# Key exponentials taken by ScalarE from PSUM with the maximum as bias, in the feature map of a linear-attention and mixture-of-experts kernel

## The chip, the cores and the metric

One Trainium2 chip, one core of it. The metric is the device time of one execution in microseconds (us); the median of several executions is given. A profiled execution is a separate one and has a time of its own. TensorE (PE) multiplies matrices and writes to PSUM, VectorE (DVE) and ScalarE (ACT) read PSUM, GpSimd (POOL) works in SBUF and issues indirect transfers, SyncE (SP) issues the other transfers. Each engine runs its own list of instructions in order; semaphores tie the lists together.

## The reference

```
def phi(x):
    proj = np.einsum('bhsd,df->bhsf', x, w_phi)
    proj = proj - np.max(np.abs(proj), axis=-1, keepdims=True)
    return np.concatenate([np.exp(proj), np.exp(-proj)], axis=-1)
q_p, k_p = (phi(q), phi(k))
kv = np.einsum('bhsf,bhsd->bhfd', k_p, v)
z = np.sum(k_p, axis=2)
num = np.einsum('bhsf,bhfd->bhsd', q_p, kv)
den = np.einsum('bhsf,bhf->bhs', q_p, z)[..., None] + 1e-06
x = (num / den)          # then, token by token: a router over 8 experts,
...                      # h = relu(x @ w1[e]); out = p[e] * (h @ w2[e])
```

Batch 8, 8 heads, 576 tokens, head dimension 64, 128 features; the model dimension is 512, there are 8 experts with a hidden width of 1024. Everything is fp32. For each token and head the kernel thus needs the maximum of the absolute projections, and four sets of 128 exponentials: of the shifted projection and of its negative, for q and for k.

## The kernel before

The first stage is the attention. Two batches and two heads form a unit of 9 chunks of 128 tokens (1152 tokens, of which chunk 4 holds tokens of both batches); there are 16 units. The stage runs in 72 steps of two chunks each. Step p, in the function `step`, does on TensorE, in this order (the TensorE order of this stage is the order of the code; a scheduler sets that of the other engines):

- `proj(p)`: 8 matmuls (16 instructions each of weight load and matmul in the profile, since fp32 takes two) give the projections of k and q, two heads and two chunks, into a tile `pj` of two PSUM banks, one bank for each head. There are two such tiles in turn. VectorE then takes the maximum of absolute values (`m`, 8 columns) and subtracts it (`sb`), ScalarE takes the key features `kp` as two exponentials.
- `qtr(p-1)`: 8 instructions transpose the shifted q of the step before, `sb`, back into the same `pj` tile; ScalarE turns that into the query features `qp` (`qexp`), 2 exponentials.
- turns: where a sum over keys was finished in the step before, 4 more transposes of it (`kvs`) into the same tile; ScalarE copies them to `ks`.
- `kv4` (chunk 4 alone), gates, `kv`: the keys' features times v are summed into `kvp`. Where such a sum is complete, ScalarE copies it to `kvs` (`kv_end`). A gate, one step after a turn, is 8 instructions of TensorE and a small ScalarE copy into `kvs`.
- up to 18 entries of the list `todo`: the numerators and denominators `nm`, which VectorE divides (`rc`, `xo`).

Spread over the later steps are the router's steps, transfers that POOL issues behind a small copy named `tick`, and in the last of the 72 steps eight splits of expert weights (a ScalarE cast to `whi`, then four POOL subtractions to `wlo`). After the 72 steps come the experts' layers, for which TensorE is nearly always busy.

In the listing below and in all profile rows of the kernel before, line 277 is the projections, 280 the maximum, 282 the subtraction, 286 the key exponentials, 295 the transposes, 310 the query exponentials, 327 and 340 the sums over keys, 361, 362 and 385 the copies into `kvs`, 374 the copy to `ks`, 405 the numerators.

Of the kernel before, what the change touches and what calls it, by code (L numbers as in the profile page):

```python
# [7 lines left out]
F32 = mybir.dt.float32  # L8
# [3 lines left out]
AF = mybir.ActivationFunctionType  # L12
ALU = mybir.AluOpType
AX = mybir.AxisListType
# [12 lines left out]
MID, DEN = slice(10, 10 + 2 * D), slice(9, 11 + 2 * D, 2 * D + 1)  # L27
# [28 lines left out]
class Kernel:  # L56
# [209 lines left out]
    def proj(self, p):  # L266

        dve, act = self.dve, self.act

        t = self.psf.tile([128, 2, 2, 2, 128], F32, name="pj")  # L270
        for i in (2 * p, 2 * p + 1):
            kq = self.g[i // 3]["kq"]
            s = slice(i % 3 * 128, i % 3 * 128 + 128)
            for j in (0, 1):
                for h in (0, 1):
                    r = slice(64 * h, 64 * h + 64)
                    self.last_pe = self.pe.matmul(t[:, h, i % 2, j, :], kq[r, j, s], self.w2[r], start=True, stop=True)  # L277
        m = self.m = self.front3.tile([128, 8], F32, name="m")
        f = t.rearrange("p h c j f -> p (h c j) f")
        dve.tensor_reduce(m, f, AX.X, ALU.max, apply_absolute_value=True)  # L280
        sb = self.front3.tile([128, 2, 2, 2, 128], F32, name="sb")
        self.last_dve = dve.tensor_sub(sb.rearrange("p h c j f -> p (h c j) f"), f,  # L282
                                       m.unsqueeze(2).broadcast_to([128, 8, 128]))
        kp = self.front3.tile([128, 2, 2, 2, 128], F32, name="kp", bufs=4)
        for sg in (0, 1):
            self.last_act = act.activation(kp[:, :, :, sg, :].rearrange("p c h f -> p h c f"), sb[:, :, :, 0], AF.Exp,  # L286
                                           scale=1.0 - 2 * sg)
        for c in (0, 1):
            self.ch[2 * p + c] = dict(kp=kp[:, c], sb=sb, pj=t.rearrange("p h c j f -> p h (c j f)"))

    def halves(self, t, a, src):

# [4 lines left out]
    def qtr(self, p):  # L297

        sb, pj = self.ch[2 * p]["sb"], self.ch[2 * p]["pj"]
        for h in (0, 1):  # L300
            for c in (0, 1):
                self.halves(pj, h * 128 + c * 64, sb[:, h, c, 1, :])
        return pj

    def qexp(self, p, pj):

        qp = self.feat.tile([128, 2, 2, 256], F32, name="qp")
        src = pj[:, :, 0:256].rearrange("p r (a k) -> p a r k", k=64)
        for sg in (0, 1):
            self.act.activation(qp[:, sg].rearrange("p h (c r k) -> p (h c) r k", c=2, r=2), src, AF.Exp,  # L310
                                scale=1.0 - 2 * sg)
        for c in (2 * p, 2 * p + 1):
            self.ch[c]["qp"] = qp
# [41 lines left out]
    def kv_end(self, u, b, t):  # L355


        hp = u % NHP
        kvs = self.back2.tile([128, 2, 2 * (KV + D + 1)], F32, name="kvs", bufs=3)
        with self.tc.high_priority():  # L360
            self.act.copy(kvs[:, :, MID].rearrange("p s (h d) -> p s h d", h=2), t[:, :, :, 0:D])
            self.act.copy(kvs[:, :, DEN], t[:, :, :, D])
        e = {}

        def turn(t):
            for sg in (0, 1):
                self.halves(t, 256 + sg * 64, kvs[:, sg, MID])
            self.gates.append(gate)
            return copy

        def copy(t):
            e["ks"] = self.back2.tile([128, 2, 128], F32, name="ks")
            with self.tc.high_priority():
                self.act.copy(e["ks"].rearrange("p s (r k) -> p s r k", r=2),
                              t[:, :, 256:384].rearrange("p r (s k) -> p s r k", s=2))

        def gate():

            t = self.psb.tile([128, 512], F32, name="nm")
            g = t[:, 476:512].rearrange("p (s h e) -> p s h e", s=2, h=2)  # L380
            for sg in (0, 1):
                for r in (slice(0, 64), slice(64, 128)):
                    self.pe.matmul(g[r, sg], e["ks"][:, sg, r], self.wgi[:, hp], start=True, stop=True)
            with self.tc.high_priority():
                self.act.copy(kvs.rearrange("p s (h x) -> p s h x", h=2)[:, :, :, 0:9], g)
            for k, cs in enumerate(((0, 1), (2, 3)) if b == 0 else ((4, 5, 6), (7, 8))):
                self.num(u, b, cs, kvs, None if k else t)
            if b == 1 and hp == NHP - 1:
                self.todo.append(lambda: self.ends(u // NHP))
        self.turns.append(turn)  # L390

    def num(self, u, b, cs, kvs, bank=None):
# [92 lines left out]
    def step(self, p, n):  # L485

        if p < n // 2:
            self.proj(p)
        gates, self.gates = self.gates, []
        turns, self.turns = self.turns, []  # L490
        q = 0 <= p - 1 < n // 2
        if q:
            pj = self.qtr(p - 1)
        elif turns:
            pj = self.psf.tile([128, 2, 512], F32, name="pj")
        copies = [x(pj) for x in turns]
        if q:
            self.small_ps = [pj[:, r, 384:512] for r in (0, 1)]
        self.chores()
        if q:  # L500
            self.qexp(p - 1, pj)
        for x in copies:
            x(pj)
        pair = (2 * (p - KVLAG), 2 * (p - KVLAG) + 1) if 0 <= p - KVLAG < n // 2 else ()
        for i in pair:
            if i % NC == 4:
                self.kv4(i)
        for x in gates:
            x()
        for i in pair:  # L510
            if i % NC != 4:
                self.kv(i)
        for _ in range(min(QUOTA, len(self.todo)) if p < n // 2 else len(self.todo)):
            self.todo.pop(0)()
# [523 lines left out]
    def tokens(self, slots, late=False):  # L1038

        for s in slots:  # L1040
            if "xg" not in s:
                self.gather_x(s)
        units, g = [(s, k) for s in slots for k in range(s["n"])], 1 if late else 4

        def step(group):
            if late:
                self.whole(*group[0], group[0][1] % 3 == 2, self.here())
                return
            out = []
            for n, (s, k) in enumerate(group):  # L1050
                if n % 2 == 0:
                    t = self.halfbanks()
                c = slice(n % 2 * 256, n % 2 * 256 + 256)
                out.append((s, k, t[:, :, c]))
                self.rows(out[-1][2], s["xg"][k])
            for s, k, t in out:
                self.unrow(s, *self.into(s), k * 128, t)
        return [lambda a=a: step(units[a:a + g]) for a in range(0, len(units), g)]
# [295 lines left out]
```

## Time and profile before

| | |
|---|---|
| median of 3 executions | 752.32 us (751.82 to 754.76) |
| profiled execution, its time | 757.47 us |
| profiled execution, its span | 755.6 us |
| TensorE matmul busy | 730.0 us, 97% of the span |
| VectorE busy | 452.1 us, 60% |
| ScalarE busy | 341.4 us, 45% |
| POOL busy | 181.7 us, 24% |
| granted TensorE clock, mean | 0.996 |
| first and last projection matmul start | 4.2 us and 284.1 us |

The profiled execution is 5.2 us (0.7%) above the median. Shares are averages over two different stages: the attention up to about 285 us, the experts after that. A row of the timeline gives start, length, engine, line, operation and tiles; PEld is TensorE's weight load, which precedes its matmul and overlaps others; idle time before a row and what ended it stand in brackets.

### The profile page before, as it was taken

How to read it: one execution, taken by the hardware profiler on the slowest of the kernel's cores; microseconds unless marked ns; L12 is line 12 of the kernel's file. 1: busy time of each engine (PE TensorE's matmuls, PEld its weight loads, DVE VectorE, ACT ScalarE, POOL GpSimd, SP SyncE). 2: the span in 40 equal slices, each digit the busy share in tenths (PEclk: the TensorE clock that was granted, in tenths of full speed). 3: DMA queues.
4: the chain of work that ended last, by engine and by line, in shares of the span. 5: the costliest groups of instructions: out<-in, count | busy, mean ns of one | idle time of the engine just before them, and what ended most of it. 6: DMA issues, size and time to landing. Idle time of an engine off the chain costs nothing. (4 is left out here: it accounts for less than half of the span.)

```text
span 755.6 us, 22152 instructions
## 1 busy us (share of the span) xinstructions
PE 730.0 (97%) x9447; PEld 632.3 (84%) x9447; DVE 452.1 (60%) x828; ACT 341.4 (45%) x644; POOL 181.7 (24%) x306
## 2 busy tenths in 40 slices
PE   7999999999998899989999999999999999999996
PEld 6999989989887788869887985889888778888995
DVE  5888888788877886583736335435522365543513
ACT  4777666666677574322424225332322255251301
POOL 0210103410364674344403130021212102101011
PEclk9999999999999999999999999999999999999999
DMA  6755545554666651054737966434686264334110
GB/s 203 239 170 146 150 128 148 136 153 129 196 194 195 197 163 54 7 170 142 262 120 284 333 249 203 164 126 140 237 299 239 98 233 167 139 126 154 57 39 29
DMA packets 66101, 125.05 MB, mean 166 GB/s; under 512 B 7220, under 2 KB 45300, under 8 KB 65950
## 3 DMA queue, kind: packets, MB, share of 16 engines
q1 hardware_dynamic: 57808, 101.03, 42.1%
q0 software_dynamic: 8016, 22.51, 8.5%
q8 instruction: 75, 1.23, 0.7%
q14 instruction: 26, 0.21, 0.1%
q10 hardware_dynamic: 176, 0.07, 0.0%
HBM read 102.05 MB, written 22.06 MB: 164 GB/s over the span
## 5 line engine op out<-in xcount | busy, mean ns | idle before, releaser
L1128 ACT ACTIVATE hh<-l 128x384 fp32r<-128x384 f32 (+1 forms) x84 | 45.2, 538 | 209.5 <-PE l L1085 160.8
L1083 PE MATMUL l<-xhi,whi 128*128 128x384 f32 (+2 forms) x352 | 124.0, 353 | 0.0
L1085 PE MATMUL l<-xhi,wlo 128*128 128x384 f32 (+2 forms) x352 | 123.6, 351 | 0.0
L1084 PE MATMUL l<-xlo,whi 128*128 128x384 f32 (+2 forms) x352 | 123.4, 351 | 0.0
L1129 DVE SCALAR_TENSOR_TENSOR hl<-l,hh 128x384 fp32r<-128x384 f32 (+1 forms) x84 | 51.6, 615 | 117.3 <-ACT hh L1128 110.8
L1083 PE MATMUL l<-whi,hh 128*128 128x512 f32 x288 | 116.2, 403 | 2.4 <-DVE y L1182 2.4
L1084 PE MATMUL l<-wlo,hh 128*128 128x512 f32 x288 | 114.4, 397 | 0.0
L1085 PE MATMUL l<-whi,hl 128*128 128x512 f32 x288 | 114.2, 396 | 0.0
L963 DVE TENSOR_TENSOR wlo<-wraw,whi 128x1024 fp32r<-128x1024 f32 x80 | 96.5, 1223 | 28.2 <-ACT whi L960 27.2
L286 ACT ACTIVATE kp<-sb 128x512 f32<-128x512 f32 x144 | 83.5, 625 | 58.2 <-DVE sb L282 54.5
L280 DVE TENSOR_REDUCE m<-pj 128x8 f32<-128x1024 f32 x72 | 87.8, 1219 | 35.3 <-PE pj L277 33.8
L960 ACT CAST whi<-wraw 128x1024 fp32r<-128x1024 f32 x88 | 90.3, 1045 | 38.1 <-PE l L1085 16.5
L277 PE MATMUL pj<-first,kq 64*128 64x128 f32 x1152 | 85.8, 290 | 8.0 <-DMA kq<-in_kqT 4.2
L310 ACT ACTIVATE qp<-pj 128x512 f32<-128x512 f32 x144 | 79.7, 594 | 24.9 <-PE pj L295 12.9
L282 DVE TENSOR_TENSOR sb<-pj,m 128x1024 f32<-128x1024 f32 x72 | 88.1, 1223 | 3.5
L405 PE MATMUL nm<-kvs,qp 128*64 128x74 f32 x2304 | 88.0, 228 | 2.1 <-issue 1.0
L277 PEld LDWEIGHTS pj<-first,kq 64*128 64x128 f32 x1152 | 72.0, 192 | 15.3 <-issue 5.2
L405 PEld LDWEIGHTS nm<-kvs,qp 128*64 128x64 f32 x2304 | 80.1, 136 | 3.4 <-issue 1.6
L327 PE MATMUL kvp<-v,kp 128*64 128x65 f32 x2048 | 78.7, 226 | 0.9 <-issue 0.4
L1185 POOL DMA_INDIRECT out<-y,p_tokm x30 | 35.0, 1166 | 181.7 <-DVE y L1182 165.2
L327 PEld LDWEIGHTS kvp<-v,kp 128*64 128x64 f32 x2048 | 67.9, 139 | 5.5 <-ACT kp L286 1.4
L1083 PEld LDWEIGHTS l<-xhi,whi 128*128 128x128 f32 x352 | 66.2, 188 | 7.1 <-issue 1.6
(224 smaller groups left out, 910.2 us busy)
## 6 DMA issues: line engine op xcount, KB each, us to landing
wraw<-in_w1h SPq DMA_DIRECT2D x44, 512.0 KB
wraw<-in_w2h SPq DMA_DIRECT2D x44, 512.0 KB
kq<-in_kqT SPq DMA_DIRECT2D x47, 384.0 KB
v<-in_va SPq DMA_DIRECT2D x48, 195.0 KB
xs<-xo SPq DMA_DIRECT2D x48, 128.0 KB
whi<-in_w1h SPq DMA_DIRECT2D x8, 512.0 KB
wlo<-in_w1h SPq DMA_DIRECT2D x8, 512.0 KB
whi<-in_w2h SPq DMA_DIRECT2D x8, 512.0 KB
```

What stands on the lines that cost most here:

```text
L277: self.last_pe = self.pe.matmul(t[:, h, i % 2, j, :], kq[r, j, s], self.w2[r], start=True, stop=True)
L280: dve.tensor_reduce(m, f, AX.X, ALU.max, apply_absolute_value=True)
L282: self.last_dve = dve.tensor_sub(sb.rearrange("p h c j f -> p (h c j) f"), f, m.unsqueeze(2).broadcast_to([128, 8, 128]))
L286: self.last_act = act.activation(kp[:, :, :, sg, :].rearrange("p c h f -> p h c f"), sb[:, :, :, 0], AF.Exp, scale=1.0 - 2 * sg)
L310: self.act.activation(qp[:, sg].rearrange("p h (c r k) -> p (h c) r k", c=2, r=2), src, AF.Exp, scale=1.0 - 2 * sg)
L327: self.pe.matmul(t[r, sg, h], kp[:, h, sg, r], v[:, h], start=first and sg + h == 0, stop=last and sg + h == 2)
L405: self.last_num = self.pe.matmul(e["t"][r, c - c0, k], self.ch[i]["qp"][:, sg, h, q0 + r.start:q0 + r.stop], kvs[:, sg, k], start=sg == 0, ...
L960: self.act.copy(hi, raw)
L963: (low or self.dve).tensor_sub(lo[:, c], raw[:, c], hi.bitcast(F32)[:, c])
L1083: mm(o, ah, bh, start=first, stop=False)
L1084: mm(o, ah, bl, start=False, stop=False)
L1085: self.last_pe = mm(o, al, bh, start=False, stop=last)
```

## The change

The tile `pj` is laid out anew: within each head's bank the two chunks of k now come first (columns 0 to 255) and the two chunks of q after them (256 to 511). VectorE still takes the maximum over all 1024 columns, but subtracts it for q only. POOL makes the negative of the maximum (`mneg`). The key features are eight ScalarE exponentials of 128 x 128 straight from PSUM, four with `m` and four with `mneg` as the bias column, in place of two of 128 x 512 from `sb`. The transposes of q go to columns 256 to 511, the turns to 128 to 255, the router's small results to 0 to 127.

```
-  self.last_pe = self.pe.matmul(t[:, h, i % 2, j, :], kq[r, j, s], self.w2[r], start=True, stop=True)
+  self.last_pe = self.pe.matmul(t[:, h, j, i % 2, :], kq[r, j, s], self.w2[r], start=True, stop=True)
   m = self.m = self.front3.tile([128, 8], F32, name="m")
-  f = t.rearrange("p h c j f -> p (h c j) f")
-  dve.tensor_reduce(m, f, AX.X, ALU.max, apply_absolute_value=True)
-  sb = self.front3.tile([128, 2, 2, 2, 128], F32, name="sb")
-  self.last_dve = dve.tensor_sub(sb.rearrange("p h c j f -> p (h c j) f"), f,
-                                 m.unsqueeze(2).broadcast_to([128, 8, 128]))
+  dve.tensor_reduce(m, t.rearrange("p h j c f -> p (h j c) f"), AX.X, ALU.max, apply_absolute_value=True)
+  nm = self.front3.tile([128, 8], F32, name="mneg")
+  self.pool.tensor_scalar_mul(nm, m, -1.0)
+  sb = self.front3.tile([128, 2, 2, 128], F32, name="sb")
+  mq = m.rearrange("p (h j c) -> p h j c", h=2, j=2)[:, :, 1]
+  self.last_dve = dve.tensor_sub(sb, t[:, :, 1], mq.unsqueeze(3).broadcast_to([128, 2, 2, 128]))
   kp = self.front3.tile([128, 2, 2, 2, 128], F32, name="kp", bufs=4)
-  for sg in (0, 1):
-      self.last_act = act.activation(kp[:, :, :, sg, :].rearrange("p c h f -> p h c f"), sb[:, :, :, 0], AF.Exp,
-                                     scale=1.0 - 2 * sg)
+  for sg in (1, 0):
+      for c in (0, 1):
+          for h in (0, 1):
+              b = (nm, m)[sg][:, h * 4 + c:h * 4 + c + 1]
+              self.last_act = act.activation(kp[:, c, h, sg], t[:, h, 0, c], AF.Exp, scale=1.0 - 2 * sg, bias=b)
...
-  self.halves(pj, h * 128 + c * 64, sb[:, h, c, 1, :])
+  self.halves(pj, 256 + h * 128 + c * 64, sb[:, h, c])
...
-  src = pj[:, :, 0:256].rearrange("p r (a k) -> p a r k", k=64)
+  src = pj[:, :, 256:512].rearrange("p r (a k) -> p a r k", k=64)
...
-  self.halves(t, 256 + sg * 64, kvs[:, sg, MID])
+  self.halves(t, 128 + sg * 64, kvs[:, sg, MID])
```

In the built program the waits move as well. The rows below are the instructions of one engine in their order; the number after a tile's name is its buffer, and the brackets name the semaphores that an instruction waits for (`DVE_49`, `Activation_49`, `PE_49` and `Pool_49` are those of the engines, `DMAHW` those of transfers).

TensorE in two steps of the second unit, before: `pj_591` and `pj_673` are the projections of two steps in a row, `sb_602` the shifted projections of the first, `kp_604` its key features.

```order
L277 MATMUL pj_673<-first_62,kq_421 128x128 [waits DMAHW3_49,PE_49,Activation_49]
L277 MATMUL pj_673<-first_62,kq_421 128x128 x7
L295 MATMUL pj_591<-first_62,sb_602 128x64 [waits DVE_49]
L295 MATMUL pj_591<-first_62,sb_602 128x64 x7
L383 MATMUL nm_700<-wgi_68,ks_622 64x18 [waits DVE_49,PE_49]
L383 MATMUL nm_700<-wgi_68,ks_622 64x18 x3
L327 MATMUL kvp_536<-v_290,kp_604 64x65 [waits Activation_49]
L327 MATMUL kvp_536<-v_290,kp_604 64x65 x3
L327 MATMUL kvp_536<-v_290,kp_604 64x65 [waits Activation_49]
```

The same place in the changed program, where the tiles are `pj_745`, `pj_655`, `sb_668` and `kp_670`.

```order
L277 MATMUL pj_745<-first_62,kq_469 128x128 [waits DMAHW3_49,PE_49,Activation_49]
L277 MATMUL pj_745<-first_62,kq_469 128x128 x7
L298 MATMUL pj_655<-first_62,sb_668 128x64 [waits DVE_49,Activation_49]
L298 MATMUL pj_655<-first_62,sb_668 128x64 x7
L386 MATMUL nm_780<-wgi_68,ks_694 64x18 [waits DVE_49,PE_49]
L386 MATMUL nm_780<-wgi_68,ks_694 64x18 x3
L330 MATMUL kvp_600<-v_322,kp_670 64x65 x16
```

The wait for ScalarE has moved from the sums over keys to the transposes of q ahead of them. Its count in the built program is the one that ScalarE reaches with the eighth key exponential of that tile, here and in 66 of the 72 steps; the transposes write other columns of the same bank.

ScalarE at the same place before: `qp_697` and `qp_783` are query features, `ks` and `kvs` the copies named above.

```order
L310 ACTIVATE qp_697<-pj_591 128x512 [waits PE_49]
L385 COPY kvs_567<-nm_700 128x4x9 [waits PE_49]
L310 ACTIVATE qp_697<-pj_591 128x512
L361 COPY kvs_722<-kvp_536 128x2x128 [waits PE_49]
L362 COPY kvs_722<-kvp_536 128x2x2 [waits Activation_49]
L286 ACTIVATE kp_686<-sb_684 128x2x2x128 [waits DVE_49]
L286 ACTIVATE kp_686<-sb_684 128x2x2x128
L310 ACTIVATE qp_783<-pj_673 128x512 [waits PE_49]
L310 ACTIVATE qp_783<-pj_673 128x512
L374 COPY ks_786<-pj_673 128x256
```

ScalarE at that place in the changed program.

```order
L313 ACTIVATE qp_777<-pj_655 128x512 [waits PE_49]
L388 COPY kvs_631<-nm_780 128x4x9 [waits PE_49]
L313 ACTIVATE qp_777<-pj_655 128x512
L364 COPY kvs_802<-kvp_600 128x2x128 [waits PE_49]
L290 ACTIVATE kp_760<-pj_745,m_754 128x128 [waits DVE_49]
L365 COPY kvs_802<-kvp_600 128x2x2 [waits Activation_49]
L290 ACTIVATE kp_760<-pj_745,m_754 128x128 x3
L290 ACTIVATE kp_760<-pj_745,mneg_756 128x128 [waits Pool_49]
L290 ACTIVATE kp_760<-pj_745,mneg_756 128x128 x3
L313 ACTIVATE qp_871<-pj_745 128x512 [waits PE_49]
```

Two exponentials have become eight, four of which wait for POOL; the count that the first of them waits for on VectorE is that of the subtraction for q, one above that of the maximum. Everything else keeps its place.

More of the change, by code (lines that the diff above doesn't have):

```diff
@@ L276, in proj @@
                     r = slice(64 * h, 64 * h + 64)
-                    self.last_pe = self.pe.matmul(t[:, h, i % 2, j, :], kq[r, j, s], self.w2[r], start=True, stop=True)
+                    self.last_pe = self.pe.matmul(t[:, h, j, i % 2, :], kq[r, j, s], self.w2[r], start=True, stop=True)
         m = self.m = self.front3.tile([128, 8], F32, name="m")
-        f = t.rearrange("p h c j f -> p (h c j) f")
-        dve.tensor_reduce(m, f, AX.X, ALU.max, apply_absolute_value=True)
-        sb = self.front3.tile([128, 2, 2, 2, 128], F32, name="sb")
-        self.last_dve = dve.tensor_sub(sb.rearrange("p h c j f -> p (h c j) f"), f,
-                                       m.unsqueeze(2).broadcast_to([128, 8, 128]))
-        kp = self.front3.tile([128, 2, 2, 2, 128], F32, name="kp", bufs=4)
-        for sg in (0, 1):
-            self.last_act = act.activation(kp[:, :, :, sg, :].rearrange("p c h f -> p h c f"), sb[:, :, :, 0], AF.Exp,
-                                           scale=1.0 - 2 * sg)
+        dve.tensor_reduce(m, t.rearrange("p h j c f -> p (h j c) f"), AX.X, ALU.max, apply_absolute_value=True)
[4 more added lines that the diff above has]
+        self.last_dve = dve.tensor_sub(sb, t[:, :, 1], mq.unsqueeze(3).broadcast_to([128, 2, 2, 128]))
+        kp = self.front3.tile([128, 2, 2, 2, 128], F32, name="kp", bufs=4)
+        for sg in (1, 0):
[3 more added lines that the diff above has]
+                    self.last_act = act.activation(kp[:, c, h, sg], t[:, h, 0, c], AF.Exp, scale=1.0 - 2 * sg, bias=b)
         for c in (0, 1):
-            self.ch[2 * p + c] = dict(kp=kp[:, c], sb=sb, pj=t.rearrange("p h c j f -> p h (c j f)"))
+            self.ch[2 * p + c] = dict(kp=kp[:, c], sb=sb, pj=t.rearrange("p h j c f -> p h (j c f)"))
     def halves(self, t, a, src):
@@ L374, in copy @@
                 self.act.copy(e["ks"].rearrange("p s (r k) -> p s r k", r=2),
-                              t[:, :, 256:384].rearrange("p r (s k) -> p s r k", s=2))
+                              t[:, :, 128:256].rearrange("p r (s k) -> p s r k", s=2))
         def gate():
@@ L497, in step @@
         if q:
-            self.small_ps = [pj[:, r, 384:512] for r in (0, 1)]
+            self.small_ps = [pj[:, r, 0:128] for r in (0, 1)]
         self.chores()
```

## The prediction

> **What bounds the kernel now.** I read the page, then the busy times by stage, the timeline of two quiet steps, the groups of instructions, and last who waits for the operations that change.
>
> ```profile
> span 755.6 us, 22152 instructions
> PE 730.0 (97%) x9447; PEld 632.3 (84%) x9447; DVE 452.1 (60%) x828; ACT 341.4 (45%) x644; POOL 181.7 (24%) x306
> core 0: us, PE busy (x) PEld busy (x) DVE busy (x) ACT busy (x) POOL busy (x), PEclk, DMA share, GB/s
> 6.00:285.00 279.00, 268.08 (x6740) 248.41 (x6737) 234.00 (x450) 187.32 (x416) 83.51 (x200) 1.00 0.58 169
> L277 PE MATMUL pj<-first,kq x1152: 272/272/578, 4.2 to 284.1; 64*128 64x128 f32 x192
> ```
>
> TensorE is the bound in both stages. In the attention, 6 to 285 us, it is busy for 268.1 of 279.0 us, VectorE for 234.0, ScalarE for 187.3 and POOL for 83.5. The projections run from 4.2 to 284.1 us. The 16 instructions of a last step take about 0.9 us, so the 71 steps between the first and the last start take 279 us, 3.93 us each. The stage is what the change can touch; the experts follow it and would only shift.
>
> Nine quiet steps (two units), here by weight loads, with no router work in them:
>
> ```profile
> 54.02 0.97 PEld L277 LDWEIGHTS pj<-first,kq 64*128 64x128 f32 x16 [0.25 <-ACT ks L374]
> ...
> 87.25 0.97 PEld L277 LDWEIGHTS pj<-first,kq 64*128 64x128 f32 x16 [0.25 <-ACT ks L374]
> ```
>
> (87.25 - 54.02) / 9 = 3.69 us a step. That is TensorE's own work, with hardly a wait. Over 71 steps it makes 262 us; the other 17 us are the start, the router's instructions and the waits that they cause. One step and a half from a later stretch:
>
> ```profile
> 142.78 0.97 PEld L277 LDWEIGHTS pj<-first,kq 64*128 64x128 f32 x16
> 143.67 0.38 PEld L295 LDWEIGHTS pj<-first,sb 64*128 64x128 f32 x8
> 144.06 1.22 DVE L280 TENSOR_REDUCE m<-pj 128x8 f32<-128x1024 f32 x1 [0.54 <-PE pj L277]
> 144.35 1.09 ACT L310 ACTIVATE qp<-pj 128x512 f32<-128x512 f32 x2 [0.43 <-PE pj L295]
> 145.32 0.38 ACT L374 COPY ks<-pj 128x256 f32<-128x256 f32 x1
> 145.39 1.23 DVE L282 TENSOR_TENSOR sb<-pj,m 128x1024 f32<-128x1024 f32 x1
> 146.48 0.97 PEld L277 LDWEIGHTS pj<-first,kq 64*128 64x128 f32 x16
> 146.65 1.15 ACT L286 ACTIVATE kp<-sb 128x512 f32<-128x512 f32 x2 [0.95 <-DVE sb L282]
> 147.36 0.38 PEld L295 LDWEIGHTS pj<-first,sb 64*128 64x128 f32 x8
> 148.09 1.21 DVE L280 TENSOR_REDUCE m<-pj 128x8 f32<-128x1024 f32 x1
> 148.42 0.19 ACT L385 COPY kvs<-nm 128x36 f32<-128x36 f32 x1
> 148.49 0.62 ACT L310 ACTIVATE qp<-pj 128x512 f32<-128x512 f32 x1
> 149.34 1.22 DVE L282 TENSOR_TENSOR sb<-pj,m 128x1024 f32<-128x1024 f32 x1
> ```
>
> The reader is to see the slack. Projections of step p start at 142.78; the subtraction ends at 146.62 and the transposes of that q stand at 147.36, after the next projections (0.89 us): 0.74 us to spare. The key exponentials run from 146.65 to 147.80, beside the projections and the transposes, before the sums over keys need them. Both paths just fit under TensorE.
>
> **VectorE's part.** The subtraction shrinks to 512 columns. The rows nearest in size are the divisions:
>
> ```profile
> L425 DVE TENSOR_TENSOR xo<-nm,rc 128x296 f32<-128x296 f32 x48 | 22.3, 465 | 2.1
> L425 DVE TENSOR_TENSOR xo<-nm,rc 128x444 f32<-128x444 f32 x16 | 9.9, 620 | 0.9
> L286 ACT ACTIVATE kp<-sb 128x512 f32<-128x512 f32 x144 | 83.5, 625 | 58.2 <-DVE sb L282 54.5 <-issue 3.3
> L310 ACT ACTIVATE qp<-pj 128x512 f32<-128x512 f32 x144 | 79.7, 594 | 24.9 <-PE pj L295 12.9 <-DVE g_cr L591 3.8 <-DVE g_es L618 3.6
> L374 ACT COPY ks<-pj 128x256 f32<-128x256 f32 x32 | 12.1, 377 | 2.1 <-PE pj L295 2.1
> L648 ACT ACTIVATE g_ex<-g_ls 128x72 f32<-128x72 f32 x4 | 1.0, 254 | 4.8 <-DVE g_ls L646 4.8
> ```
>
> 620 - 465 ns for 148 columns is 1.05 ns a column, so 512 take 620 + 71 = 0.69 us where 1.23 stood. VectorE saves 72 x 0.54 = 39 us of busy time, beside a TensorE that is the bound; on the path it shortens the way to `sb` by 0.54 us.
>
> **ScalarE's part.** Two exponentials (1.15 us together) become eight of 128 columns. From 512 and 256 columns, (594 - 377) / 256 = 0.85 ns a column, so 128 columns from PSUM last 377 - 109 = 268 ns. Consecutive rows overlap by about 0.1 us: two of 594 end after 1.09, and the copy at 148.42 lasts 0.19 but the next row starts 0.07 later. No row shows an exponential with a bias column. Call K the time of the eight. Low end: all overlap and the column is free, 8 x 0.17 + 0.1 = 1.46. High end: the smallest exponential, 254 ns for 72 columns, carried to 128 (254 + 48 = 302) with no overlap, 2.41. I take eight whole durations of the nearest size, 8 x 0.27 = 2.16, that is, the bias column costs what the overlap saves. The Trainium skill ("ScalarE: Activation LUTs", section "What ACT_TABLE_LOAD costs") says that an exponential with a per-partition column as bias takes 280 ns + 0.833 ns a column and that neighbours overlap by 93 ns; K would be 8 x 294 + 93 ns = 2.44 us, and the time below about 812. No run here shows such a bias; for constants it gives 186 + 426 = 612 ns at 512 columns, and the trace's 625 agrees.
>
> **The moved wait.** The transposes of q now wait for all eight, though they need only `sb` and write other columns. The first exponential waits for the subtraction, so nothing of the k path starts earlier than `sb`. The Trainium skill ("PSUM — Partial Sum Buffer", section "PSUM bank collisions raise a hardware error") has such a rule: two engines must be kept apart by bank and 32 partitions, whatever the columns. Were the columns enough, ScalarE would carry 0.97 + 2.16 and 0.31 of copies, 3.44 us a step, under TensorE's 3.69, and the time would stay near 752; the built program has the wait in 66 of 72 steps, so the sum goes by it. Queued behind the transposes on TensorE are the gates, the sums over keys, the numerators and the next projections: whatever the transposes wait is lost to TensorE. Two loops follow.
>
> Loop one, over two steps. Projections to maximum 144.06 - 142.78 = 1.28, maximum to subtraction 149.34 - 148.09 = 1.25, subtraction 0.69, to ScalarE 0.03, K, to TensorE 0.05: transposes 3.30 + K after their projections. From transposes to the next projections but one 146.48 - 143.67 = 2.81. So two steps cannot be shorter than 6.11 + K: 4.14 us a step at K = 2.16, where TensorE's work is 3.69.
>
> Loop two, on ScalarE, from transposes to transposes: `qp` starts 0.68 later where a turn follows (143.67 to 144.35) and runs 0.97 until the next row; `ks` 0.28; K; 0.05. That is 1.98 + K = 4.14 in the four of nine steps that have a `ks`. The four of nine that copy `kvs` must first have the sum over keys:
>
> ```profile
> 96.88 0.46 PE L295 MATMUL pj<-first,sb 64*128 64x64 f32 x8 [0.30 <-DVE sb L282]
> ...
> 97.53 0.32 PEld L340 LDWEIGHTS kvp<-v,kp 64*64 64x64 f32 x16 [0.34 <-ACT kp L286]
> ...
> 99.42 0.37 ACT L361 COPY kvs<-kvp 128x256 f32<-128x256 f32 x1 [0.31 <-PE kvp L327]
> ...
> 105.51 0.41 PE L295 MATMUL pj<-first,sb 64*128 64x64 f32 x8
> ...
> 107.54 0.36 ACT L361 COPY kvs<-kvp 128x256 f32<-128x256 f32 x1
> ```
>
> The copy starts 2.54 - 0.34 = 2.20 after the transposes in the first case (the wait for `kp` in it would be gone), 2.03 in the second; with 0.28 for it, 0.06 for the small copy and 0.05, these steps take 2.59 + K = 4.75 and 2.42 + K = 4.58. In the two others the sum is done before ScalarE is free, 2.0 + K = 4.16; the ninth step is held by loop one. Mean: (5 x 4.14 + 2 x 4.16 + 4.58 + 4.75) / 9 = 4.26 us, 0.57 over TensorE's work, or 40.5 us in 71 steps.
>
> **POOL's part and the rest.** `mneg` is one small POOL instruction a step, like the `tick` copy below, 0.19 us; POOL is busy for 30% of the stage and the first four exponentials (1 us) cover it. Where a split of weights runs, they do not:
>
> ```profile
> L532 POOL COPY tick<-m 128x1 f32<-128x1 f32 x34 | 6.4, 189 | 51.2 <-DVE m L280 46.6 <-DVE g_mk L603 2.4 <-DVE p_rie L723 1.7
> L960 ACT CAST whi<-wraw 128x1024 fp32r<-128x1024 f32 x88 | 90.3, 1045 | 38.1 <-PE l L1085 16.5 <-DMA wraw<-in_w2h 11.2 <-DMA wraw<-in_w1h 7.6
> L963 POOL TENSOR_TENSOR wlo<-wraw,whi 128x256 fp32r<-128x256 f32 x32 | 22.4, 731 | 8.4 <-ACT whi L960 8.4
> PEld kvp L340: 2.8, 11
> PEld kvp L327: 1.4, 7
> PE kvp L340: 1.0, 5
> DVE sb L282: 7.1, 14
> ```
>
> A cast (1.0) and four POOL rows (2.8) then stand between the exponentials of one step and `mneg` of the next; with 0.2 for that and K / 2 for the last four, such a step takes about 5.1 in place of 4.3: eight of them, +7 us. The last four rows above are TensorE's present waits for `kp` and `sb`, 12.3 us in all. The first three go into the moved wait; of the 17 us above TensorE's work I let 6 be absorbed by the longer steps, the rest (start, router work on VectorE inside loop one) stays. Fetches, numerators and `xs` transfers move along with TensorE.
>
> Sum: 40.5 + 7 - 6 = +41.5 us on the profiled execution, 757.5 to 799.0. That execution stands 5.2 above the median of the runs, 752.3, which gives 794.
>
> **Rivals.**
> The exponentials overlap fully and the column is free, K = 1.46: loop one is 3.79, the two late `kvs` steps 3.88 and 4.05, mean 3.83, +10; POOL's part halves, 6 is absorbed: +7.5, 760. For it: the overlap of present rows. Against: eight column reads at no cost.
> The exponentials cost 2.41: loop one 4.26, `ks` steps 4.39, the `kvs` steps 4.41, 4.41, 4.83, 5.00, mean 4.50, +57.5, +1 for the rest: 811, and 817 if nothing is absorbed. For it: the small exponential's row.
> Faster: VectorE's relief decides. With K under 1.27 loop one is below TensorE's 3.69, the transposes wait for nothing, and the 12.3 us of present waits can return: 740. It needs 0.16 us an exponential, below any row's spacing at that width.
> No change: K near the low end with POOL's part hidden and all excess absorbed, within 4 us of 752. What changes by less than 0.5%, about 4 us, cannot be told from nothing.
>
> **Chances.** Main case 0.50, cheap exponentials 0.18, dear ones 0.22, faster 0.05, no change 0.05. The range 757 to 818 runs from just under the second case to the end of the third; under 2 in 10 lie outside, by the two last cases and by costs beyond the ends. Faster 0.05, same 0.05, slower 0.90.
>
> **What would show it.** The eight rows of `kp` at 128x128 of 0.27 us or more, some 2.2 us for a set; the transposes' idle time put down to ScalarE's `kp`, about 0.5 us in most steps; quiet steps of 4.2 to 4.3 in place of 3.69; TensorE's share in the attention near 85%; the last projections near 325 us and the experts' stage as long as before; VectorE's busy time down by 39. I am wrong if the transposes start 0.89 after the projections as now, or if the eight take under 1.3 us.

## The result and the profile after

The change makes the kernel slower: 799.7 us (median of 4 executions, 798.3 to 800.4) against 752.1 (4 executions, 750.9 to 754.8) for the kernel before on the same chip, a ratio of 1.0625 with a 95% interval of 1.0609 to 1.0641. Forecast were 794 us, with a range from 757 to 818. The profiled execution took 799.98 us where that of before took 757.47: +42.5 against +41.5 forecast. The medians lie further apart, 47.6 us, because the profiled execution of before lay 5.4 us above the median of its 4 and that of after only 0.3 above its own.

The page of the changed kernel: the span, the busy times, and the granted clock in 40 slices.

```profile
span 798.1 us, 22762 instructions
PE 738.2 (92%) x9447; PEld 635.3 (80%) x9447; DVE 418.3 (52%) x828; ACT 410.5 (51%) x1076; POOL 200.0 (25%) x378
PEclk8999999999999989999999999999999999999999
```

VectorE lost 33.8 us of busy time and ScalarE gained 69.1; what TensorE does stayed nearly the same, but its share of the span fell from 97% to 92%. Next the attention in the same window as before (its columns are the stretch, its length, busy time of PE, PEld, DVE, ACT and POOL, clock, DMA share, GB/s), then the projections and the subtraction by line.

```profile
6.00:285.00 279.00, 241.45 (x5892) 218.87 (x5890) 176.29 (x390) 222.42 (x736) 74.32 (x216) 0.98 0.50 146
L277 PE MATMUL pj<-first,kq x1152: 272/272/579, 4.2 to 330.3; 64*128 64x128 f32 x192
L284 DVE TENSOR_TENSOR sb<-pj,m x72: 669/691/693, 7.6 to 332.0; 128x512 f32<-128x512 f32 x72
```

TensorE is busy for 241.5 of 279 us where it was for 268.1. ScalarE, the engine that got the work, is at 222 of 279 and so is not full. The last projections start at 330.3 instead of 284.1, +46.2 us; from there to the end of the span it is 467.8 us instead of 471.5. All of the loss therefore lies in the attention. Steps 15 to 24, the same quiet nine as those of the prediction:

```profile
64.02 0.97 PEld L277 LDWEIGHTS pj<-first,kq 64*128 64x128 f32 x16 [0.26 <-ACT ks L377]
...
101.89 0.97 PEld L277 LDWEIGHTS pj<-first,kq 64*128 64x128 f32 x16 [0.25 <-ACT ks L377]
```

(101.89 - 64.02) / 9 = 4.208 us a step, where it was 3.692. Who waits for whom (total us, times, longest):

```profile
PEld pj L298 <- ACT kp L290: 44.1, 57, 2.8
PE pj L298 <- ACT kp L290: 32.3, 46, 2.6
ACT kp L290 <- POOL mneg L281: 5.1, 7, 0.9
```

The transposes of q (line 298) now sit 44 us, in 57 of 72 steps, behind the key exponentials, counted by their weight loads; the second line is the same waits once more, counted by their matmuls. Before, the weight loads waited 4.6 us for `sb` there. The prediction's row of 7.1 us adds the waits of the matmuls to that. One step of the timeline and the groups of the exponentials show the size of K:

```profile
151.58 0.69 DVE L284 TENSOR_TENSOR sb<-pj,m 128x512 f32<-128x512 f32 x1
152.30 1.14 ACT L290 ACTIVATE kp<-pj,m 128x128 f32<-128x128 f32 x4
152.81 0.97 PEld L277 LDWEIGHTS pj<-first,kq 64*128 64x128 f32 x16
153.32 1.16 ACT L290 ACTIVATE kp<-pj,mneg 128x128 f32<-128x128 f32 x4
154.53 0.33 PEld L298 LDWEIGHTS pj<-first,sb 64*128 64x128 f32 x8 [0.75 <-ACT kp L290]
L290 ACT ACTIVATE kp<-pj,m 128x128 f32<-128x128 f32 x288 | 85.8, 388 | 10.0 <-DVE sb L284 9.5
L290 ACT ACTIVATE kp<-pj,mneg 128x128 f32<-128x128 f32 x288 | 84.6, 412 | 5.1 <-POOL mneg L281 5.1
```

The eight run from 152.30 to 154.48, K = 2.18 us; the transposes start 0.05 after them, though the projections ahead of them were issued by 153.78 and `sb` was ready at 152.27. A single row lasts 0.39 to 0.41 us, not 0.27, but consecutive rows start only about 0.26 us apart.

### The profile page after: what moved, and what is told of

Same layout as the page of the kernel before. It is cut to its first block, busy times and chain, and to the rows that moved or that the text cites. A ratio compares the mean times of both kernels' runs of the same rounds, so it can differ in the third digit from the quotient of the medians.

```text
span 798.1 us, 22762 instructions
## 1 busy us (share of the span) xinstructions
PE 738.2 (92%) x9447; PEld 635.3 (80%) x9447; DVE 418.3 (52%) x828; ACT 410.5 (51%) x1076; POOL 200.0 (25%) x378
## 3 DMA queue, kind: packets, MB, share of 16 engines
q8 instruction: 75, 1.23, 0.6%
## 5 line engine op out<-in xcount | busy, mean ns | idle before, releaser
L313 ACT ACTIVATE qp<-pj 128x512 f32<-128x512 f32 x144 | 81.0, 607 | 47.3 <-PE pj L298 33.8
L277 PE MATMUL pj<-first,kq 64*128 64x128 f32 x1152 | 87.4, 294 | 17.3 <-ACT qp L313 9.4
L290 ACT ACTIVATE kp<-pj,m 128x128 f32<-128x128 f32 x288 | 85.8, 388 | 10.0 <-DVE sb L284 9.5
L290 ACT ACTIVATE kp<-pj,mneg 128x128 f32<-128x128 f32 x288 | 84.6, 412 | 5.1 <-POOL mneg L281 5.1
L330 PEld LDWEIGHTS kvp<-v,kp 128*64 128x64 f32 x2048 | 69.1, 142 | 3.5 <-issue 0.6
```

The costliest lines, as they stand in the source:

```text
L277: self.last_pe = self.pe.matmul(t[:, h, j, i % 2, :], kq[r, j, s], self.w2[r], start=True, stop=True)
L290: self.last_act = act.activation(kp[:, c, h, sg], t[:, h, 0, c], AF.Exp, scale=1.0 - 2 * sg, bias=b)
L330: self.pe.matmul(t[r, sg, h], kp[:, h, sg, r], v[:, h], start=first and sg + h == 0, stop=last and sg + h == 2)
```

## The experiments

The experiments ran on other chips than the pair above; the kernel before took 757.2 to 757.8 us there, so ratios are compared, and within the traces the mean of steps 15 to 24 ("quiet step") and the start of the last step's weight loads.

**1. Eight exponentials, but from SBUF.** In the kernel before, with its layout and its whole subtraction; `zc` is a column of zeros. The transposes do not wait for `kp` here, so this is ScalarE's part without the moved wait.

```
-  for sg in (0, 1):
-      act.activation(kp[:, :, :, sg, :]..., sb[:, :, :, 0], AF.Exp, scale=1.0 - 2 * sg)
+  for sg in (0, 1): for c in (0, 1): for h in (0, 1):
+      act.activation(kp[:, c, h, sg], sb[:, h, c, 0], AF.Exp, scale=1.0 - 2 * sg, bias=self.zc[:, 0:1])
```

> The kernel before, with the key features taken by eight exponentials of 128 columns with a (zero) bias column, but from the shifted projections in SBUF as before. The eight cost ScalarE as much as in the changed kernel (K about 2.2 us), and the transposes of q wait for the subtraction alone. Theory A (the moved wait: the eight stand in the loop from transposes to transposes): near 752 us, at most 8 more where the sums over keys wait for the last exponentials. Theory B (the work itself: ScalarE carries 1.1 us more a step): near 795, as the changed kernel.

Measured: 790.35 us, ratio 1.0436 (1.0414 to 1.0458); quiet step 4.00. One set of eight takes 2.45 us. The rows of ScalarE and TensorE in one stretch:

```profile
143.90 2.45 ACT L290 ACTIVATE kp<-sb,zc 128x128 f32<-128x128 f32 x8 [0.45 <-DVE sb L284]
144.62 0.41 PE L299 MATMUL pj<-first,sb 64*128 64x64 f32 x8
146.11 0.64 PE L344 MATMUL kvp<-v,kp 64*64 64x65 f32 x16 [0.53 <-ACT kp L290]
146.26 1.05 ACT L314 ACTIVATE qp<-pj 128x512 f32<-128x512 f32 x2
148.33 0.37 ACT L365 COPY kvs<-kvp 128x256 f32<-128x256 f32 x1 [0.66 <-PE kvp L331]
148.60 0.41 ACT L290 ACTIVATE kp<-sb,zc 128x128 f32<-128x128 f32 x1
```

The transposes pass at once, at 144.62. But `qp`, which could start when they end at 145.03, stands behind `kp` until 146.26. And ScalarE does not fill the gap: the sum over keys waits for `kp`, the copy of `kvs` waits 0.66 us for that sum, and the next `kp` stands behind the copy until 148.60. The next rows list what ended TensorE's idle time before the projections here (us, times; the idle of weight loads and that of matmuls are added, though they overlap), first the projections' own line.

```profile
L279 PE MATMUL pj<-first,kq x1152: 272/272/579, 4.1 to 314.2; 64*128 64x128 f32 x192
ACT ks L378: 21.2, 27
ACT qp L314: 13.0, 8
```

Before, these two were 7.0 and 0.6 us. The projections two steps on need the bank that `qp` and `ks` still read. So eight dear exponentials cost 30 us of attention even where the transposes are free. Theory A, at most 8 us more, failed: the run takes 32.6 us more than the kernel before, near theory B.

**2. The same with fewer or no bias columns.** In `const_from_sb` the eight have no bias column, in `mix_from_sb` five of them have one.

```
-                 bias=self.zc[:, 0:1])
+                 )                                      # const_from_sb
+                 **kw)   # mix_from_sb: kw = bias=self.zc[:, 0:1] for the first five, else nothing
```

> The kernel before with eight exponentials of 128 columns from the shifted projections, no bias column: K about 1.7 us, no moved wait; the result is the reference's. Its counterpart with the moved wait and K 1.47 ended its projections 14 us later than the kernel before. Theory A (moved wait): the 14 us go, 0 to 4 us over the kernel before. Theory B (ScalarE's queue alone, whatever waits): 14 us or more, since its eight are longer here than there.

> As the one above, with a zero bias column on five of the eight: K about 2.1 to 2.2 us, as in the changed kernel, no moved wait. ScalarE carries 0.97 + 2.1 + 0.31 = 3.4 us a step of TensorE's 3.69. With K 2.45 it was 33 us over the kernel before. Theory A as predicted (3.4 is under 3.69, nothing waits): 0 to 6 us over. Theory B' (without the moved wait the eight stand ahead of the query features in ScalarE's queue, and the projections two steps on wait for these): 12 to 25 us over; the changed kernel's remaining 20 to 35 us are then the moved wait's.

Measured: without columns 767.48 us, ratio 1.0135 (1.0105 to 1.0164), quiet step 3.77; with five 783.96 us, 1.0356 (1.0327 to 1.0384), 3.93. One set of each, and then the idle time of mix_from_sb's projections:

```profile
63.91 1.71 ACT L290 ACTIVATE kp<-sb 128x128 f32<-128x128 f32 x8 [0.81 <-DVE sb L284]
...
68.89 1.57 ACT L291 ACTIVATE kp<-sb,zc 128x128 f32<-128x128 f32 x5 [0.81 <-DVE sb L284]
...
70.37 0.69 ACT L291 ACTIVATE kp<-sb 128x128 f32<-128x128 f32 x3
ACT ks L378: 17.8, 26
ACT qp L314: 5.9, 7
```

The second set takes 70.37 + 0.69 - 68.89 = 2.17 us, the same K as in the changed kernel. It thus shows what this K costs without the moved wait: the last step starts at 305.5 us instead of 283.2, 22.3 later, of the 46.2 that the changed kernel loses. Neither run met its expectation: const_from_sb is 9.7 us over the kernel before, between theory A (0 to 4) and theory B (14 or more), and mix_from_sb is 26.2 over, a little more than theory B' allowed (12 to 25).

**3. From PSUM without a bias column.** These two leave out the maximum for k (and `mneg`), so `kp` is not shifted. Their tokens go to other experts, and the second stage runs longer than in any other kernel here; only the attention is read from them. One has two exponentials of 512 as before, the other eight of 128.

```
-  b = (nm, m)[sg][:, h * 4 + c:h * 4 + c + 1]
-  act.activation(kp[:, c, h, sg], t[:, h, 0, c], AF.Exp, scale=1.0 - 2 * sg, bias=b)
+  act.activation(kp[:, :, :, sg, :]..., t[:, :, 0], AF.Exp, scale=1.0 - 2 * sg)     # two_from_bank
+  act.activation(kp[:, c, h, sg], t[:, h, 0, c], AF.Exp, scale=1.0 - 2 * sg)        # eight_no_bias
```

> The changed kernel with two exponentials of 512 columns straight from the banks and no bias (the maximum is left out for k, and no negative is made on POOL). The transposes of q still wait for them. Theory A: K is 1.1 us, loop one (6.11 + 1.1) / 2 = 3.6 us, under TensorE's 3.69; only steps with a late sum reach 3.7: 750 to 760 us. Theory C (the wait as such, the layout, or ScalarE reading the banks beside TensorE's writes): 780 or more, at any K.

> The changed kernel with its eight exponentials but no bias column (the maximum is left out for k, no negative on POOL). Theory A with a price on the column: each lasts 0.27 us, start to start 0.17, K 1.5, mean step 3.83 to 3.9: 758 to 770 us. Rival (the column is free and the 0.39 us of a row are due to the source or the width): rows stay at 0.39, K 2.2, about 795.

Measured: 907.09 and 919.75 us in all (ratios 1.1969 and 1.2134, not comparable). In the attention, first the set, the projections and the moved wait of two_from_bank, then those of eight_no_bias:

```profile
60.41 1.09 ACT L285 ACTIVATE kp<-pj 128x512 f32<-128x512 f32 x2
L277 PE MATMUL pj<-first,kq x1152: 272/272/577, 4.2 to 287.5; 64*128 64x128 f32 x192
PEld pj L294 <- ACT kp L285: 6.1, 12, 1.2
```

```profile
62.29 1.47 ACT L287 ACTIVATE kp<-pj 128x128 f32<-128x128 f32 x8
L277 PE MATMUL pj<-first,kq x1152: 272/272/580, 4.3 to 298.2; 64*128 64x128 f32 x192
PEld pj L295 <- ACT kp L287: 13.8, 25, 2.1
```

With K = 1.09 the moved wait is there and costs little: the last projections at 287.5, +3.4, quiet step 3.71; theory C, a dear wait at any K, is out. With K = 1.47 the last projections start 14.1 later than before and the quiet step is 3.80. The bias column thus costs (2.18 - 1.47) / 8 = 0.09 us an exponential. These 0.71 us are about two thirds of the 1.09 us by which K grows from two_from_bank to the changed kernel.

**4. Two exponentials more.** The changed kernel with two further ones of a k block into a tile that nobody reads.

```
+  ex = self.front3.tile([128, 2, 128], F32, name="ex")
+  for h in (0, 1):
+      self.last_act = act.activation(ex[:, h], t[:, h, 0, 0], AF.Exp, bias=nm[:, h * 4:h * 4 + 1])
```

> The changed kernel with two more exponentials with a bias column in each step (a copy of two that are made anyway, into a tile that nothing reads): K about 2.7 us. Theory A (loops with K in them): the mean step grows by 0.5 x 0.7 to 0.5, so 25 to 37 us over the changed kernel, 72 to 84 over the kernel before. A theory in which the loss comes from the layout or POOL: no more than 10 us over the changed kernel.

Measured: 836.17 us, ratio 1.1058 (1.1009 to 1.1106), as expected 78 us over the kernel before; quiet step 4.63. The first of the set's rows starts at 90.34, the last row ends at 93.05: K = 2.71. TensorE's wait now names the added ones:

```profile
90.34 1.17 ACT L290 ACTIVATE kp<-pj,m 128x128 f32<-128x128 f32 x4
...
92.35 0.70 ACT L293 ACTIVATE ex<-pj,mneg 128x128 f32<-128x128 f32 x2
PEld pj L301 <- ACT ex L293: 68.7, 63, 2.8
```

Two instructions whose result nobody uses lengthen the step by 0.42 us for 0.53 us of K: ScalarE's time up to its last read of the bank is what the step waits for.

**5. The layout alone.** The new columns, with the whole subtraction and the two exponentials from SBUF.

```
-  dve.tensor_sub(sb, t[:, :, 1], mq.unsqueeze(3).broadcast_to([128, 2, 2, 128]))
+  dve.tensor_sub(sb..., t.rearrange("p h j c f -> p (h j c) f"), m.unsqueeze(2).broadcast_to([128, 8, 128]))
...
+  act.activation(kp[:, :, :, sg, :]..., sb[:, :, 0], AF.Exp, scale=1.0 - 2 * sg)
```

> The changed layout of the banks (k and q apart) with the work of the kernel before: one subtraction of 1024 columns, two exponentials from the shifted projections in SBUF, no moved wait. If the layout itself costs or gains nothing: within 0.4% of the kernel before. If the transposes into another half of the bank, or the strided reads, cost something: outside of it.

Measured: 757.07 us, ratio 0.9998 (0.9981 to 1.0015), quiet step 3.69. The layout costs nothing.

**6. The negative on VectorE.**

```
-  self.pool.tensor_scalar_mul(nm, m, -1.0)
+  dve.tensor_scalar_mul(nm, m, -1.0)
```

> The changed kernel with the negative of the maximum made by VectorE in place of POOL. The prediction put 7 us on POOL's queue (weight splits ahead of the negative): by it 792 to 794 us. Rival (POOL's queue is covered elsewhere, and VectorE's extra 0.15 us a step lies ahead of the subtraction or behind it): 798 to 806.

Measured: 804.79 us, ratio 1.0644 (1.0621 to 1.0668), overlapping the changed kernel's 1.0625. The transposes wait for `kp` about as long as in the changed kernel: 44.9 us in 61 steps. Taking POOL off the path brought no gain that can be measured. VectorE does 72 more rows of 0.17 us here and the quiet step is 4.24, so that a gain of some 2 us could be hidden.

**7. Four exponentials and a reciprocal.** exp(x) as 1 / exp(-x), so that four exponentials and `mneg` fall away.

```
-  for sg in (1, 0): ...
+  act.activation(kp[:, c, h, 1], t[:, h, 0, c], AF.Exp, scale=-1.0, bias=m[...])    # four of them
+  dve.reciprocal(kp[:, :, :, 0], kp[:, :, :, 1])
```

> The changed kernel with four exponentials, of the negative with m as bias; the others are their reciprocals, made by VectorE, and POOL makes no negative. K about 1.14 us, the moved wait stays. VectorE gains about 0.6 us a step, to 3.3 of 3.7 us. Theory A: as with the two exponentials without a bias, whose projections ended 3 us after those of the kernel before: 2 to 15 us over the kernel before, the upper part if the sums over keys wait for the reciprocals. Theory C (wait or layout as such, at any K): 40 or more over.

Measured: 972.69 us, ratio 1.2847 (1.2812 to 1.2882), a miss. The group says why:

```profile
L288 DVE RECIPROCAL kp<-kp 128x512 f32<-128x512 f32 x72 | 241.1, 3348 | 31.7 <-ACT kp L286 30.7
```

The reciprocal of 512 columns takes 3.35 us, 6.5 ns a column, where the subtraction of as many took 0.69. VectorE became the bound, with a quiet step of 6.86 us; on K this run says nothing.

**8. The first two steps as before.** The changed kernel loses 2.1 us by its third step and 10.0 by its fifteenth; a drop of the clock falls into the third.

```
+  if p < 2:   # whole subtraction, two exponentials from SBUF
...
+  else:       # as in the changed kernel
```

> The changed kernel, with the first two steps alone done as in the kernel before (subtraction for k and q, two exponentials from SBUF). In the changed kernel 16 exponentials stand ahead of the first query features, TensorE idles 2.85 and 1.07 us, and its granted clock is 0.50 from 13.6 to 17.6 us; 6 us of the loss lie in the first 13 steps beyond what quiet steps explain. If that start is the cause: 4 to 6 us less than the changed kernel, a ratio of 1.055 to 1.058 against its 1.0625. If the later steps take the place (each loop catches up with a start that was early): no less than 1.061.

Measured: 801.41 us, ratio 1.0586 (1.0551 to 1.0621): it overlaps the changed kernel's 1.0609 to 1.0641. In its trace step 15 starts at 60.73 instead of 64.02, but the last at 329.96 instead of 329.40. The start's 3.3 us came back later in that one execution; the ratio lies between the two expectations, and the run settles nothing about the total.

**9. The copies to VectorE.** `ks` and `kvs` copied by VectorE, which has room, so that ScalarE's list shrinks.

```
-  self.act.copy(e["ks"]..., ...);  self.act.copy(kvs[:, :, MID]..., ...);  self.act.copy(kvs[:, :, DEN], ...)
+  self.dve.tensor_copy(...)        # the same three
```

> The changed kernel with the copies ks and kvs (not the small one of a gate) made by VectorE, which is idle for nearly half of it. If the length of ScalarE's loop sets the steps (ks 0.28 in four of nine, kvs 0.34 in four of nine, 0.27 a step): loop one then holds, quiet steps of 4.1, 6 to 15 us less than the changed kernel. If loop one (VectorE's maximum and subtraction, then the eight) or the wait for late sums holds instead: within 4 us of it, or slower where a copy delays the maximum.

Measured: 795.87 us, ratio 1.0512 (1.0476 to 1.0548), the best of the changed kernel's variants and still slower than before. By the ratios that is 8.6 us less than the changed kernel, within the 6 to 15 that were expected of a shorter ScalarE list, but the quiet step is 4.22, unchanged, where 4.1 was expected. In steps 15 to 24 every set starts within 0.22 us of the end of its subtraction here, so ScalarE's list hardly holds it back, and the step is still as long. In exchange VectorE's copies delay a subtraction, in step 15 by 0.9 us. Loop one, with the moved wait in it, thus seems to be enough to make the step as long as it is.

The gain lies behind these steps. At step 24 the two kernels are level, 101.65 and 101.89 us; the last step starts at 321.8 here and at 329.4 there. First what ended the projections' idle time here, then the row for `qp` of the changed kernel (weight loads and matmuls added, as above; "issue" is idle time that ended with nothing that the profile shows):

```profile
issue: 12.6, 12
DVE ks L377: 8.4, 16
ACT qp L313: 1.0, 2
```

```profile
ACT qp L313: 19.5, 10
```

Now ScalarE's order in one step, the 28th: first the changed kernel, with the projections of the 29th, then this run, last the kernel before.

```profile
122.75 0.60 ACT L313 ACTIVATE qp<-pj 128x512 f32<-128x512 f32 x1
...
124.97 1.18 ACT L290 ACTIVATE kp<-pj,mneg 128x128 f32<-128x128 f32 x4
125.96 0.66 ACT L313 ACTIVATE qp<-pj 128x512 f32<-128x512 f32 x1
126.68 1.21 PEld L277 LDWEIGHTS pj<-first,kq 64*128 64x128 f32 x16 [2.09 <-ACT qp L313]
```

```profile
122.32 1.09 ACT L313 ACTIVATE qp<-pj 128x512 f32<-128x512 f32 x2
```

```profile
107.79 0.61 ACT L310 ACTIVATE qp<-pj 128x512 f32<-128x512 f32 x1
...
108.32 1.18 ACT L286 ACTIVATE kp<-sb 128x512 f32<-128x512 f32 x2
```

In the changed kernel the second exponential of this `qp` stands behind the copies of `kvs` and all eight of the next `kp`, and the projections wait 2.09 us for it. The same order is found in 4 of its 72 steps. The projections after them wait 2.09, 2.09, 1.70 and 3.22 us, 9.1 us together; no step of this run or of the kernel before has that order. So the change moved more than the listed steps show, where everything else keeps its place. Here the copies and the order changed together, so what the order alone costs was not measured. The start is the same in both kernels: the third step begins at 13.62, and its 16 weight loads take 1.79 us here and 1.78 there.

No version that ran beats the kernel before.

## Why the prediction was right, and where it was not

**The kernels together.** K is the time of the set, the quiet step that of steps 15 to 24, the last column the start of the last step's weight loads.

| kernel | K, us | transposes wait for `kp` | quiet step, us | last step, us |
|---|---|---|---|---|
| before | 1.15 | no | 3.69 | 283.2 |
| const_from_sb | 1.71 | no | 3.77 | 291.5 |
| mix_from_sb | 2.17 | no | 3.93 | 305.5 |
| eight_from_sb | 2.45 | no | 4.00 | 313.3 |
| two_from_bank | 1.09 | yes | 3.71 | 286.7 |
| eight_no_bias | 1.47 | yes | 3.80 | 297.3 |
| after | 2.18 | yes | 4.21 | 329.4 |
| ten | 2.71 | yes | 4.63 | 361.3 |

**VectorE's part** held: the subtraction took 0.69 us as forecast, and its 72 rows 88.1 - 49.6 = 38.5 us less in all where 39 were forecast. VectorE's whole busy time fell by 33.8 only: it counts rows that overlap once. Added up row by row it fell by 38.0.

**K** held in its sum, 2.18 against 2.16, and in part in its working. Without a column the rows last 0.32 us on average in eight_no_bias and start (1.47 - 0.32) / 7 = 0.164 us apart, where the prediction had 0.17, and a set takes 1.47, its low end. The column adds 0.09 us a row, where the prediction let it cost the 0.1 that overlap saves. It had no row for that price, so that the choice came out is luck. The rows themselves are longer than its 0.27, 0.32 without and 0.39 to 0.41 with a column, and overlap by 0.13 us or more. The estimate by the Trainium skill ("ScalarE: Activation LUTs", section "What ACT_TABLE_LOAD costs") was 2.44. The eight from SBUF agree with it: 2.45 measured, and its 280 + 0.833 x 128 = 387 ns with 93 ns of overlap stand beside a row of 392 ns and a spacing of (2.45 - 0.39) / 7 = 0.294 us. From PSUM the trace says 2.18; there the measurement decides.

**The moved wait** held: its two loops gave 4.26 us for the quiet step at K = 2.16, and 4.208 was measured at 2.18. In all of steps 15 to 24 the transposes start 0.05 us after the last exponential of the set. Loop one fits best: in eight of these ten steps the first exponential starts within 0.11 us of the end of the subtraction, as that loop has it. The long steps of loop two, 4.58 and 4.75, did not come: from transposes to transposes the longest of these steps takes 4.42. At other K, by the same formulas, the prediction's cheap case has 3.83 at 1.46 (3.80 at 1.47 measured), and 2.71 makes (4.41 + 4 x 4.69 + 2 x 4.71 + 5.13 + 5.30) / 9 = 4.78 (4.63 measured). That it is nearly free below some K, as the rival "faster" had it, is borne out by two_from_bank: 3.71 at 1.09. What that rival hoped for beyond this did not come: the steps of two_from_bank are no shorter than before's. Its 12.3 us of present waits were too many as well, since weight loads and matmuls wait at the same time; the weight loads alone waited 2.8 + 1.4 + 4.6 = 8.8.

**The step that failed** is "Were the columns enough, ScalarE would carry ... 3.44 us a step, under TensorE's 3.69, and the time would stay near 752". mix_from_sb has that K and no moved wait, and takes 1.0356 of the time before. A busy sum below TensorE's is no bound for an engine that takes its list in order and whose entries wait for TensorE in turn (`qp` for transposes, `kvs` for sums over keys, which wait for `kp`). The prediction thus put the whole loss down to the moved wait, where about half of it, 22.3 of 46.2 us, arises without it. The other 24 us come in the changed kernel, but the split is not exact: mix_from_sb has the long subtraction of 1.23 us, which starts its exponentials later, and the changed kernel has the short one. And the four waits for a late `qp`, 9.1 us, are among the 24; they come from ScalarE's order rather than from the moved wait, since copies_on_dve has the wait and not these. The changed layout without the wait was not tried: the transposes would need a bank of their own. Nor does any run show what would happen if both engines worked on one bank at once; the rule of the Trainium skill that the prediction named for this was not put to a test.

**POOL's part**, +7, was not borne out. ScalarE did wait for `mneg` where the prediction had it, behind seven of the eight splits, for 0.6 to 0.9 us each, 5.1 us in all. With `mneg` on VectorE the ratio is 1.0644 against 1.0625, no gain, so that no run shows what of this TensorE lost.

**The rest** was sized +7 - 6 = +1 and came to +9.6: of the 46.2 us, 71 x 0.516 = 36.6 are quiet-step loss (40.5 forecast). Of the 9.6, 2.8 fall before step 15 (10.0 less 14 x 0.516) and 6.8 after step 24. Behind step 24 lie the four waits for the late `qp`, 9.1 us, where the kernel before waited 0.3 for `qp`; the prediction had no term for them. A part may be the clock, which the prediction left at full. The stage was cut into seven windows; these are the three in which the clock (the last figure but two) is below 1.00:

```profile
0.00:20.00 20.00, 11.60 (x146) 10.67 (x146) 6.40 (x9) 9.95 (x30) 1.33 (x9) 0.83 0.65 192
...
120.00:180.00 60.00, 53.43 (x1305) 48.65 (x1304) 37.27 (x82) 47.37 (x160) 19.29 (x55) 0.97 0.42 118
...
285.00:330.00 45.00, 35.18 (x827) 32.45 (x823) 24.41 (x60) 32.95 (x105) 25.91 (x56) 0.92 0.48 143
```

20 x 0.17 + 60 x 0.03 + 45 x 0.08 = 8.8 us of full clock were not granted, which is the most that it can have cost directly; in before the same seven windows all have 1.00. At the very start that figure says little, because the trace of before has a record of the clock only from 12.4 us on: its 16 weight loads at 11.53 us took 1.37 us instead of 0.97, under a stated 1.00. How the 9.6 us divide between the waits and the clock stays open. The 40.5 was too high by 3.9, and the rest too low by 8.6; the absorbed 6 are not seen.

**What would show it**: the transposes' idle time is put down to `kp`, 44.1 us over 72 steps or 0.61 each (0.5 forecast); TensorE's share in the window is 241.5 / 279 = 87% (85%); the last projections start at 330.3 (325); the experts' stage is 3.7 us shorter (as long as before).

The sum, +41.5 against +42.5, is so near partly because these cancel (the stage lost 46.2, and the experts gave 3.7 back). That is luck, and not the working of the prediction.

## What to carry to other kernels

Work moved to an engine with spare busy time can still lengthen a loop: add up the in-order list of that engine with what its entries wait for, not its busy time. When reads of a PSUM bank become longer, look in the order for writers of other columns of that bank, since they may have been made to wait for all of its readers. Compare the whole order of an engine before and after a change, not one step of it: here four steps of 72 had another order. Replacing one wide instruction by many narrow ones with a per-partition operand has to be priced by the start-to-start time of such rows, from a kernel that has them.

## What the runs showed that was not expected

A bias column costs ScalarE 0.09 us an exponential of 128 columns from PSUM, and (2.45 - 1.71) / 8 = 0.09 from SBUF; the source in PSUM saves 0.03 of spacing, 0.256 ((2.18 - 0.39) / 7) against 0.294.

VectorE's reciprocal takes 6.5 ns a column, about five times what the subtraction takes (0.69 us for 512).

The clock fell around single waits of 2 to 3 us of TensorE. Rows of the changed kernel:

```profile
10.58 0.33 PEld L298 LDWEIGHTS pj<-first,sb 64*128 64x128 f32 x8 [2.85 <-ACT kp L290]
13.62 1.78 PEld L277 LDWEIGHTS pj<-first,kq 64*128 64x128 f32 x16 [1.07 <-ACT qp L313]
...
295.31 1.78 PEld L277 LDWEIGHTS pj<-first,kq 64*128 64x128 f32 x16 [3.22 <-ACT qp L313]
```

The 16 weight loads took 1.78 us instead of 0.97 there, at a clock of 0.50 (13.6 to 17.6 us) and 0.54 (295.3 to 301.9 us). The first fall came before the wait of 1.07: from 10.98 to 12.55 us the clock is 0.60 already. A third fall, to 0.51 from 127.3 to 130.8 us, followed the wait of 2.09 before 126.68, but after waits of 2.09 before 206.76 and of 2.52 before 288.23 the 16 loads took 0.97. The Trainium skill ("TensorE: Matmul & The Clock Gate", section "What's actually happening") puts the drop after an idle window of about 3.4 us; the waits here are all shorter. In the 3.41 us ahead of the three falls TensorE was busy for 0.84 (from 7.88 us), 1.47 (from 123.93) and 1.04 us (from 291.19). That the clock fell is read from the rows; that the idle time was the cause was not tested by itself.
